# A first batch's token mix written straight to three rank groups, x added by TensorE, V as one piece, and a new order table

## The chip, the cores and the metric

The kernel runs on one core of one Trainium2 chip. The metric is the device time of one execution in microseconds (us). Engine names are those of the profile: PE is TensorE's matmul, PEld its weight load, DVE is VectorE, ACT ScalarE, POOL GpSimd, SP SyncE, which issues the DMAs.

## What is computed

The attention part is a recurrence over 768 positions for 4 batches and 8 heads of width 48; its result, with the heads side by side, is x with 384 channels. On x a mix over the positions of rank 32 and a feed-forward of width 1536 follow:

```python
for t in range(S):
    cur = np.einsum('bhd,bhe->bhde', u[None] * kt, vt)
    y[:, :, t] = np.einsum('bhd,bhde->bhe', rt, state + cur)
    state = wt[:, :, :, None] * state + np.einsum('bhd,bhe->bhde', kt, vt)
...
xt = x.transpose(0, 2, 1)
h = xt @ U @ V                      # U: 768 x 32, V: 32 x 768
u = x + h.transpose(0, 2, 1)
ch = np.maximum(u @ w_ch1, 0.0) @ w_ch2
return (u + ch)
```

## The kernel before

**Tiles and stages.** Each batch is cut into 6 chunks of 128 positions (chunks are numbered 0 to 23 through all batches) and into 2 blocks of 384 positions. All work is a list of named steps, and the string ORDER, which was written ahead of time, gives the order in which the steps are emitted. Every engine works through its own steps strictly in that order; a step that waits holds up all steps behind it on its engine. Three more digits of a step's entry choose between two engines where the step allows it, and how many dummy matmuls ("leads", in the function `warm`, L180) TensorE does ahead of it.

**A chunk** on its way: DVE scans the decays twice (F, L367, and Q, L380) with a reciprocal R between them; r and k are scaled (RP L387, KS L392, on DVE or POOL). For the first batch r times k is formed by PR (L448) and reduced by TensorE (MD); for later batches RK, RU and RED (L413, L416, L420) do this. TensorE makes the scores (AM, `aps`, L495), the diagonal comes from SEL and SEL2 (L430, L432), and DVE merges both with a predicated copy (CP, L498). KT, KN and DS (L482, L486, L505) make the chunk's contribution to the state, which ZA (L526) adds and ZM (L535, L537) decays. YA and YZ (L555 to L582) give the chunk's y in PSUM, XE (L598, ACT) copies it to `xT`, and XT and XN (L616, L620) turn it into `xn`, positions on partitions.

**The token mix of a batch** (`token_mix`). GA (L640) multiplies `xn` of the six chunks with U. The chunks c and c+4 go to the same 32 of 128 PSUM partitions, so that four partial sums of 32 ranks stand in `ga`. G4 (L646, ACT) copies them to SBUF, and SELM (L651, `gb`) adds the four with a matrix `sel` and puts the sum three times, on partitions 0, 32 and 64. GS (L655) rounds it to fp32r, and GSL (L660, DVE) puts the remainder in the third group.

**u of a block** (`make_u`). For each of 3 channel tiles HP (L690) multiplies `gs` with `Vst`, the three stacked groups of V (its second group holds V's remainder), UADD (L694, DVE) adds x in place in `xT`, UH (L699, ACT, or L701, DVE) rounds to fp32r in a tile `u`, and UL (L705, POOL or DVE) gives the remainder.

**The feed-forward of a block** (`ffn`). 12 tiles: UP (L738, 9 matmuls), HH (L745 or L747, relu and rounding), HL (L751, remainder). Then 3 output tiles of 36 matmuls each: DN (L774, in four parts of 9). O (L789, DVE) adds u, and OUT sends it. PSUM has three buffers `ffn` for `ga`, `gb`, `hp`, UP and DN.

**Weights** come as 64-bit words. For each piece LRAW loads it, AB and E (L261, L278, ACT) and C1, C2, C3 (L283, L290, L297, DVE) turn the bits, ADD (L304, POOL) joins them, and HI (L314, L316) and SUB (L321) split into fp32r and remainder. V is two pieces of 384 columns on 96 partitions, each loaded by three DMAs.

Of the kernel before, what the change touches and what calls it, by code (L numbers as in the profile page):

```python
# [37 lines left out]
def channel_order():  # L38
# [13 lines left out]
    "3n01g01F03p00004C01X03s03r04E03y03u03o03t03v01h01i04D01j01G04d01k00104e01I00201l01H05304F04L03q01Z01J04H01m0"  # L52
    "1K01n00z04G00301o10401Y01L03z11M00700503++3w01a04m04I01N15201b03-"
    "13x04014M042C4100+00604404304J00P00901000804K10-"
    "04605U01105B04R01c01204714g00R04n14S04h15504N04l15610A04i04V01d04504O04P14s01300G04W01e04j04X10h04804Q11f15T"
    "04k04T05700I05C14f04905804t00i04A00B01405u00k04B00C00j04o00l05c05W04w04p04q15D00m05X01515d16105Y05914U04r15b"
    "04u00Q05E05A00n05H04v00D00o00q04Y05I05Z00E01600S08O05i05a05400T00s05x04Z05j05e00U01805v05y14x05F04a05z08X00F"
    "05J05f14y10V04b05L00r05+00Y04z04c05G14+06218Y08o05V00p10W06304-08P05K06001705g18y01905k05-"
    "00a01A00t05O05h11B00u00X15P06405w08x00v05005l08p01C05Q05100w06511y05R05M05p05N02x05S08Z15m06618R06E08Q00H05q"
# [927 lines left out]
```

## Time and profile before

| what | value |
|---|---|
| median of 3 runs (lowest to highest) | 483.46 us (481.89 to 484.27) |
| the profiled execution's own time | 483.14 us |
| its span in the profile | 481.4 us |
| PE, PEld busy | 449.4 us (93%), 409.8 us (85%) |
| DVE, ACT, POOL busy | 314.6 us (65%), 171.2 us (36%), 119.9 us (25%) |
| first matmul of the feed-forward | 81.77 us after the span's start |
| DMA read | 41.94 MB |

The profile is of one execution. Busy shares are means over the whole span, and the stages differ: until the first feed-forward matmul the chunks of batch 0 and the first weights are prepared, and from then on feed-forward matmuls and the chunks of later batches share TensorE. A row of a timeline gives start, length, engine, line of code, operation and tiles; in square brackets stands the idle time before it and what ended it.

### The profile page before, as it was taken

The numbers are of one execution on the slowest core, as the hardware profiler recorded it, in microseconds if no ns is written. First come the engines' busy times: TensorE is split into PE (matmuls) and PEld (weight loads), VectorE is DVE, ScalarE is ACT, GpSimd is POOL, SyncE is SP. The second block draws the span as 40 slices with busy tenths as digits, with TensorE's granted clock in tenths as the row PEclk, the third lists the DMA queues.
The fourth block names the chain that finished last, engine by engine and source line by source line (L and its number), as shares of the span: only waits on it lengthen the run. The fifth ranks groups of instructions, "written<-read, shape, count | busy, mean of one in ns | idle before, by whom it ended". The sixth has DMA issues, their size and how long they took to land.

```text
span 481.4 us, 9783 instructions
## 1 busy us (share of the span) xinstructions
PE 449.4 (93%) x4041; PEld 409.8 (85%) x4041; DVE 314.6 (65%) x532; ACT 171.2 (36%) x446; POOL 119.9 (25%) x113
## 2 busy tenths in 40 slices
PE   7568797899999999999999999999999999999994
PEld 3357655799889889899999889799999899999994
DVE  8998999997999888967139558954134144422420
ACT  5485967874524532432044451320011121001000
POOL 3515422534643664402006050600000010000000
PEclk9786999999999999999999999999999999999999
DMA  8653867344105873214024360200000000000001
GB/s 301 226 193 93 298 212 252 116 146 157 38 23 154 251 216 90 75 43 130 18 83 149 100 218 34 84 20 1 33 18 0 19 17 18 0 34 16 1 17 39
DMA packets 20644, 47.38 MB, mean 98 GB/s; under 512 B 2480, under 2 KB 8880, under 8 KB 20592
## 3 DMA queue, kind: packets, MB, share of 16 engines
q1 hardware_dynamic: 20592, 46.67, 30.3%
q8 instruction: 34, 0.56, 0.5%
q14 instruction: 18, 0.15, 0.1%
HBM read 41.94 MB, written 4.72 MB: 97 GB/s over the span
## 4 chain that ended last, share of the span: by engine, by line
PE 70%; DVE 16%; DMA 5%; ACT 4%; issue 3%; POOL 1%; SPq 0%; ACTq 0%; DVEq 0%; POOLq 0%
PE f L774 29%; PE f L738 28%; PE aps L495 3%; DVE F L367 3%; DVE A L498 2%; DMA v<-in_vN 2%; PE y L555 2%; DVE cva_w L297 1%; DMA raw_w<-in_w 1%; PE trk L482 1%; DVE Q L380 1%; PE y L565 1%; PE trx L616 1%; DMA rk<-in_rkT 1%; DVE cva_w L283 1%
## 5 line engine op out<-in xcount | busy, mean ns | idle before, releaser
L738 PE MATMUL f<-u,w1h 128*128 128x384 f32 x576 | 157.0, 343 | 1.6 <-DVE u L705 0.8
L738 PEld LDWEIGHTS f<-u,w1h 128*128 128x128 f32 x576 | 105.3, 188 | 4.5 <-DVE u L705 1.5
L774 PE MATMUL f<-hh,w2h 128*128 128x384 f32 x288 | 99.4, 345 | 0.7 <-DVE hl L751 0.5
L774 PE MATMUL f<-hh,w2l 128*128 128x384 f32 x288 | 97.7, 339 | 0.7 <-POOL w2l L321 0.7
L738 PE MATMUL f<-u,w1l 128*128 128x384 f32 x288 | 97.5, 338 | 0.0
L751 DVE SCALAR_TENSOR_TENSOR hl<-f,hh 128x384 fp32r<-128x384 f32 x96 | 52.7, 552 | 34.9 <-ACT hh L745 33.7
L745 ACT ACTIVATE hh<-f 128x384 fp32r<-128x384 f32 x52 | 25.2, 486 | 137.6 <-PE f L738 137.5
L774 PE MATMUL f<-hl,w2h 128*128 128x384 f32 x288 | 66.7, 339 | 0.1
L774 PEld LDWEIGHTS f<-hh,w2h 128*128 128x128 f32 x288 | 54.1, 188 | 3.0 <-issue 1.0
L774 PEld LDWEIGHTS f<-hh,w2l 128*128 128x128 f32 x288 | 54.1, 188 | 1.2 <-POOL w2l L321 1.0
L738 PEld LDWEIGHTS f<-u,w1l 128*128 128x128 f32 x288 | 54.1, 188 | 0.0
L774 PEld LDWEIGHTS f<-hl,w2h 128*128 128x128 f32 x288 | 51.9, 188 | 0.5 <-DVE hl L751 0.4
L789 DVE TENSOR_TENSOR xT<-f,xT 128x384 f32<-128x384 f32 x24 | 13.3, 554 | 50.7 <-PE f L774 50.6
L747 DVE TENSOR_SCALAR hh<-f 128x384 fp32r<-128x384 f32 x44 | 24.2, 552 | 31.0 <-PE f L738 30.7
L430 ACT ACTIVATE A<-ident,dv 128x128 f32<-128x128 f32 x112 | 35.6, 392 | 24.8 <-PE y L565 16.1
L498 DVE COPY_PREDICATED A<-maskf,aps 128x1024 f32<-128x1024 uint32 x24 | 31.5, 1313 | 11.4 <-PE aps L495 5.7
L304 POOL TENSOR_TENSOR cva_w<-cva_w,raw_w 128x384 int32<-128x384 int32 x24 | 28.3, 1182 | 42.1 <-DVE cva_w L297 16.7
L432 POOL TENSOR_SCALAR_AFFINE_SELECT A<-dv 128x512 f32<-128x512 f32 x20 | 15.9, 804 | 75.5 <-PE y L565 58.9
L367 DVE TENSOR_TENSOR_SCAN F<-w,resets 128x517 f32<-128x517 f32 x24 | 33.4, 1399 | 1.8 <-POOL rk L392 1.3
L495 PE MATMUL aps<-rk 48*128 48x128 f32 x384 | 29.7, 297 | 3.8 <-DVE A L498 2.9
L380 DVE TENSOR_TENSOR_SCAN Q<-w,qd 128x516 f32<-128x516 f32 x24 | 32.5, 1354 | 0.1
L495 PEld LDWEIGHTS aps<-rk 48*128 48x128 f32 x384 | 25.0, 199 | 8.8 <-issue 3.7
(116 smaller groups left out, 575.7 us busy)
## 6 DMA issues: line engine op xcount, KB each, us to landing
rk<-in_rkT SPq DMA_DIRECT2D x24, 512.0 KB, 4.4
raw_w<-in_w SPq DMA_DIRECT2D x24, 384.0 KB, 4.2
kr<-in_rkN SPq DMA_DIRECT2D x18, 384.0 KB, 3.9
w<-in_wT SPq DMA_DIRECT2D x24, 258.5 KB, 2.8
v<-in_vN SPq DMA_DIRECT2D x24, 224.0 KB, 3.3
out_dram<-xT SPq DMA_DIRECT2D x24, 192.0 KB, 1.9
raw_V<-in_V SPq DMA_DIRECT2D x6, 96.0 KB, 4.2
raw_U<-in_U SPq DMA_DIRECT2D x1, 192.0 KB, 4.3
```

The costliest lines, as they stand in the source:

```text
L304: lambda: nc.gpsimd.tensor_tensor(out=d["to"].bitcast(I32), in0=d["a"].bitcast(I32), in1=d["e"], op=ALU.add),
L367: nc.vector.tensor_tensor_scan(out=F[:, ::-1], data0=st["w"][:, ::-1], data1=resets[:, ::-1], initial=1.0, op0=ALU.mult, op1=ALU.add)
L380: nc.vector.tensor_tensor_scan(out=st["Q"], data0=st["w"][:, 0:n], data1=qd, initial=0.0, op0=ALU.mult, op1=ALU.add)
L430: nc.scalar.activation(A[:, i, j], ident, AF.Copy, scale=dv[:, NP * i + j : NP * i + j + 1])
L432: nc.gpsimd.affine_select(out=A[:, i], in_=dv[:, NP * i : NP * i + NP].unsqueeze(2).broadcast_to([P, NP, P]), pattern=[[0, NP], [1, P]], c ...
L495: nc.tensor.matmul(aps[:, i, j, :], rk[r, 1, j, :], rk[r, 0, j, :], start=True, stop=True)
L498: nc.vector.copy_predicated(flat(st["A"]), mask8, flat(st["aps"]))
L738: nc.tensor.matmul(ps, wt[:, f, ct, :], u[ct][:, z], start=(n == 0), stop=(n == 8))
L745: nc.scalar.activation(hh, d["ps", f], AF.Relu)
L747: nc.vector.tensor_scalar(out=hh, in0=d["ps", f], scalar1=0.0, scalar2=None, op0=ALU.max)
L751: nc.vector.scalar_tensor_tensor(out=hl, in0=d["ps", f], scalar=0.0, in1=hh.bitcast(F32), op0=ALU.max, op1=ALU.subtract)
L774: nc.tensor.matmul(d["o", ct], wt[:, 4 * ct + part, f - 3 * part, :], hid[f][z], start=(part == 0 and n == 0), stop=(part == 3 and n == 8),)
```

## The change

**Token mix of batch 0.** GA, G4 and SELM of the first batch go. A step GW for each chunk multiplies `xn` with U three times, once for each of the three groups of `gb`, and adds up over the six chunks in PSUM. The other batches keep GA, G4 and SELM.

**u of block 0 of batch 0.** A step IX multiplies x with the identity into `hp`; HP then adds to it. UHP and ULP read `hp` in PSUM in place of `xT`, ULP is on DVE always, and XU copies `hp` to `xT` (ACT or DVE), which the output steps O wait for. The seven other blocks keep UADD, UH and UL.

**V** is one piece of 128 partitions and 192 columns, loaded by one DMA. VM copies it by identity matmuls into the three groups in PSUM (12 matmuls), HIV (ACT) rounds, SUBV (DVE) gives the remainder. HI and SUB of V go.

**`sel`** is made by three reductions instead of one and a copy.

**The order table** is new as a whole. Leads before: MD 0 31, KT 0 6, YA 5 22, XT 0.5 4, SELM 0 4, AM 6 2, YA 6 2, in all 71. Leads now: MD 0 31, YA 7 7, in all 38.

```diff
 ORDER = (
-    "3n01g01F03p00004C01X03s03r04E03y03u03o03t03v01h01i04D01j01G04d01k00104e01I00201l01H05304F04L03q01Z01J04H01m0"
...
+    "3i03k04700001S01J01b03n03j04803t04A04Z04+00200103m03p04G03o00303q04901U01T00403l04B04C01K00501V01L01M01W04Y0"
...
-    sel1 = const.tile([P, RANK], F32, name="sel1")
-    nc.vector.tensor_reduce(
-        out=sel1, in_=ident.rearrange("p (g r) -> p r g", r=RANK), op=ALU.add, axis=AX.X
-    )
-    nc.vector.tensor_copy(sel, sel1.unsqueeze(1).broadcast_to([P, 3, RANK]))
+    for i in range(3):
+        nc.vector.tensor_reduce(out=sel[:, i], in_=ident.rearrange("p (g r) -> p r g", r=RANK), op=ALU.add, axis=AX.X)
...
-            else:
-                for g in range(3):
-                    nc.sync.dma_start(flat[RANK * g : RANK * (g + 1), :], V[i].bitcast(U32))
+                nc.sync.dma_start(flat[:, 0 : 2 * NCH * RANK], (U if kind == "U" else V).bitcast(U32))
...
+                def spread(half=half):
+                    ps = d["ps", half] = psF.tile([P, TB], F32, tag="ffn", name=f"vm_{half}")
+                    lead(ps)
+                    for q in range(2):
+                        r = slice(RANK * (2 * half + q), RANK * (2 * half + q + 1))
+                        for g in range(3):
+                            nc.tensor.matmul(
+                                ps[RANK * g : RANK * (g + 1), cols * q : cols * (q + 1)], ident[:, r], d["a"],
+                                start=True, stop=True,
+                            )
+
+                def high_v(half=half, ts=ts):
+                    nc.scalar.activation(Vst[:, ts], d["ps", half][0 : 3 * RANK], AF.Copy)
+
+                def low_v(half=half, ts=ts):
+                    r = slice(RANK, 2 * RANK)
+                    nc.vector.tensor_tensor(
+                        out=Vst[r, ts], in0=d["ps", half][r], in1=Vst[r, ts].bitcast(F32), op=ALU.subtract
+                    )
...
+            def whole(c):
+                if c == 0:
+                    d["gb"] = psF.tile([P, DM], F32, tag="ffn", name=f"gb_{b}")
+                    lead(d["gb"])
+                for i in range(3):
+                    to = d["gb"][RANK * i : RANK * (i + 1), :]
+                    nc.tensor.matmul(to, U_sb[:, c, :], xns[b, c]["xn"], start=(c == 0), stop=(c == NCH - 1))
...
+            by_pe = (b, blk) == (0, 0)
+
+            def take_x(ct=ct):
+                hp = d["hp", ct] = psF.tile([P, TB], F32, tag="ffn", name=f"hp_{b}_{blk}_{ct}")
+                lead(hp)
+                nc.tensor.matmul(hp, ident, blocks[b, blk][:, ct, :], start=True, stop=False)
...
-                nc.tensor.matmul(hp, gs["gs"][:, cs], Vst[:, ts], start=True, stop=True)
+                nc.tensor.matmul(hp, gs["gs"][:, cs], Vst[:, ts], start=not by_pe, stop=True)
...
+            def keep(eng, ct=ct):
+                if eng == "ACT":
+                    nc.scalar.activation(blocks[b, blk][:, ct, :], d["hp", ct], AF.Copy)
+                else:
+                    nc.vector.tensor_copy(blocks[b, blk][:, ct, :], d["hp", ct])
...
-            o = step(f"O {b}.{blk}.{ct}", "DVE", total, [prev], use=[bps, bx])
+            o = step(f"O {b}.{blk}.{ct}", "DVE", total, [prev] + keeps, use=[bps, bx])
...
-    pieces = [("U", 0), ("V", 0)] + pieces[:8] + [("V", 1)] + pieces[8:]
+    pieces = [("U", 0), ("V", 0)] + pieces
```

What the new table does to the queues is seen at three places. The numbers in the names tell tiles apart: `hp_0_0_1` is batch 0, block 0, channel tile 1; `aps_7`, `y_7`, `Z_7` belong to chunk 7, the second of batch 1; `f1_0_0_0` is the first feed-forward tile.

On TensorE, right behind the token mix of batch 0, before (L495 is AM 6, L690 the three HP of block 0, L482 is KT 6):

```order
L495 MATMUL aps_6_961<-rk_6_660 128x128 x8
L690 MATMUL hp_0_0_0_976<-Vst_125,gs_0_958 128x384
L690 MATMUL hp_0_0_1_988<-Vst_125,gs_0_958 128x384
L690 MATMUL hp_0_0_2_990<-Vst_125,gs_0_958 128x384
L482 MATMUL trk_6_992<-ident_101,rk_6_660 128x128 x4
```

and now (L734 is IX, L743 HP, L507 KT, L520 AM, L530 DS, L641 XT):

```order
L743 MATMUL hp_0_0_0_864<-Vst_125,gs_0_1023 128x384
L743 MATMUL hp_0_1_0_1041<-Vst_125,gs_0_1023 128x384
L743 MATMUL hp_0_1_1_1045<-Vst_125,gs_0_1023 128x384
L743 MATMUL hp_0_1_2_1054<-Vst_125,gs_0_1023 128x384
L734 MATMUL hp_0_0_1_1064<-xT_0_0_395,ident_101 128x384
L743 MATMUL hp_0_0_1_1064<-Vst_125,gs_0_1023 128x384
L507 MATMUL trk_7_1068<-ident_101,rk_7_715 128x128 x4
L520 MATMUL aps_7_1081<-rk_7_715 128x128 x8
L530 MATMUL dS_120<-v_7_905,kn_7_1079 48x48 x8
L641 MATMUL trx_1_0_1106<-ident_101,xT_1_0_1091 128x128 x3
```

HP of block 1 now stands between the first and the second HP of block 0, and KT, AM and DS of chunk 7 behind them.

On TensorE, ahead of the first feed-forward matmul, before (y_6 and dS are of chunk 6):

```order
L555 MATMUL y_6_1002<-A_6_912,v_6_797 32x128 x8
L565 MATMUL y_6_1002<-A_6_912,v_6_797 32x128 x8
L616 MATMUL trx_1_0_1051<-ident_101,xT_1_0_1038 128x128 x3
L505 MATMUL dS_120<-v_6_797,kn_6_1044 48x48 x8
L738 MATMUL f1_0_0_0_1069<-u_0_0_0_1032,w1h_126 128x384
L738 MATMUL f1_0_0_0_1069<-u_0_0_0_1032,w1l_127 128x384
L738 MATMUL f1_0_0_0_1069<-u_0_0_1_1042,w1h_126 128x384
```

and now (the four rows of y_7 are YA 7 and YZ 7; L734 and L743 are IX and HP of the third channel tile; L507 is KT 8):

```order
L580 MATMUL y_7_1124<-A_7_989,v_7_905 32x128 x8
L590 MATMUL y_7_1124<-A_7_989,v_7_905 32x128 x8
L603 MATMUL y_7_1124<-rk_7_715,Z_6_1025 32x128 x8
L607 MATMUL y_7_1124<-rk_7_715,Z_6_1025 32x128 x4
L734 MATMUL hp_0_0_2_1172<-xT_0_0_395,ident_101 128x384
L743 MATMUL hp_0_0_2_1172<-Vst_125,gs_0_1023 128x384
L507 MATMUL trk_8_1185<-ident_101,rk_8_869 128x128 x4
L803 MATMUL f1_0_0_0_1196<-u_0_0_0_1119,w1h_126 128x384
L803 MATMUL f1_0_0_0_1196<-u_0_0_0_1119,w1l_127 128x384
L803 MATMUL f1_0_0_0_1196<-u_0_0_1_1149,w1h_126 128x384
```

Chunk 7, which came among the feed-forward matmuls before, now stands ahead of the first of them, and so does KT 8.

On DVE, before, from GSL of batch 0 (L660) to the second UL (L705); L694 is UADD:

```order
L660 TENSOR_TENSOR gs_0_958<-gb_0_949,gs_0_958 32x384
L420 TENSOR_REDUCE dv_7_974<-kr_7_671 128x8
L403 RECIPROCAL qd_109<-F_7_935 128x4
L498 COPY_PREDICATED A_6_912<-maskf_106,aps_6_961 128x1024
L694 TENSOR_TENSOR xT_0_0_415<-hp_0_0_2_990,xT_0_0_415 128x384
L694 TENSOR_TENSOR xT_0_0_415<-hp_0_0_1_988,xT_0_0_415 128x384
L694 TENSOR_TENSOR xT_0_0_415<-hp_0_0_0_976,xT_0_0_415 128x384
L420 TENSOR_REDUCE dv_8_1030<-kr_8_896 128x8
L380 SCALAR_TENSOR_TENSOR Q_7_1036<-w_7_648,qd_109 128x516
L705 TENSOR_TENSOR u_0_0_0_1032<-xT_0_0_415,u_0_0_0_1032 128x384
L705 TENSOR_TENSOR u_0_0_1_1042<-xT_0_0_415,u_0_0_1_1042 128x384
```

and now, the last twelve rows up to the third ULP (L761); ten rows stand between GSL and these, the first XU, two UADD of block 1, KS 7, RP 7 and weight work among them (L392 is F, L523 CP, L551 ZA, L747 UADD of block 1, L346 SUB):

```order
L392 SCALAR_TENSOR_TENSOR F_8_1093<-w_8_728,resets_87 128x517
L283 TENSOR_SCALAR cva_w2_2_1076<-cva_w2_2_1076 128x384
L428 RECIPROCAL qd_109<-F_8_1093 128x4
L523 COPY_PREDICATED A_7_989<-maskf_106,aps_7_1081 128x1024
L551 TENSOR_TENSOR Z_7_1121<-dS_120,Z_6_1025 128x384
L761 TENSOR_TENSOR u_0_0_0_1119<-hp_0_0_0_864,u_0_0_0_1119 128x384
L290 SCALAR_TENSOR_TENSOR cva_w2_2_1076<-raw_w2_2_1021,cva_w2_2_1076 128x384
L761 TENSOR_TENSOR u_0_0_1_1149<-hp_0_0_1_1064,u_0_0_1_1149 128x384
L747 TENSOR_TENSOR xT_0_1_717<-hp_0_1_2_1054,xT_0_1_717 128x384
L392 SCALAR_TENSOR_TENSOR F_9_1179<-w_9_953,resets_87 128x517
L346 TENSOR_TENSOR w1l_127<-cva_w1_4_872,w1h_126 128x384
L761 TENSOR_TENSOR u_0_0_2_1191<-hp_0_0_2_1172,u_0_0_2_1191 128x384
```

GSL and the last remainder of u were 13 rows apart on DVE with GSL counted, and are now 23, with the scans of chunks 8 and 9 and CP 7 between them.

More of the change, by code (lines that the diff above doesn't have):

```diff
@@ L310, in split_raw @@
             ready[key] = [add]
+            return
+        if kind == "V":
+            for half in range(2):
+                bps = Buf("ffn")
+                ts = slice(half * TB, (half + 1) * TB)
+                def spread(half=half):
[15 more added lines that the diff above has]
+                    )
+                vm = step(f"VM V{half}", "PE", spread, [add], take=[bps], use=[bcva])
+                hi = step(f"HIV V{half}", "ACT", high_v, [vm], use=[bps])
+                sub = step(f"SUBV V{half}", "DVE", low_v, [hi], use=[bps])
+                ready["V", half] = [hi, sub]
             return
@@ L660, in low @@
             nc.vector.tensor_tensor(out=gs[r], in0=d["gb"][r], in1=gs[r].bitcast(F32), op=ALU.subtract)
+        if b == 0:
+            sums, ga = [], None
+            def whole(c):
[5 more added lines that the diff above has]
+                    nc.tensor.matmul(to, U_sb[:, c, :], xns[b, c]["xn"], start=(c == 0), stop=(c == NCH - 1))
+            for c in range(NCH):
+                ga = step(
+                    f"GW {b}.{c}", "PE", lambda c=c: whole(c), xns[b, c]["steps"] + ready.get(("U", 0), []) + [ga],
+                    take=[bgb] if c == 0 else [], use=[bgb, xns[b, c]["buf"]],
+                )
+            hi = step(f"GS {b}", "ACT", high, [ga], take=[d["buf"]], use=[bgb])
+            d["step"] = step(f"GSL {b}", "DVE", low, [hi], use=[bgb, d["buf"]])
+            return
         ga = [
@@ L713, in make_u @@
-            xs = [s for c in range(3 * blk, 3 * blk + 3) for s in xns[b, c]["steps"] + xs_done.get((b, c), [])]
-            ad = step("UADD " + nm, "DVE", add, [hp] + xs, use=[bhp, bx])
-            uh = step(
-                "UH " + nm, "ACT", high, [ad] + ups[-1:], take=[bu], use=[bx], alt="DVE"
-            )
+                ENG[eng].tensor_tensor(out=u[:, 1], in0=summed(), in1=u[:, 0].bitcast(F32), op=ALU.subtract)
+            def keep(eng, ct=ct):
[3 more added lines that the diff above has]
+                    nc.vector.tensor_copy(blocks[b, blk][:, ct, :], d["hp", ct])
@@ new lines, in make_u @@
+            nm = f"{b}.{blk}.{ct}"
+            xs = [s for c in range(3 * blk, 3 * blk + 3) for s in xns[b, c]["steps"] + xs_done.get((b, c), [])]
+            if by_pe:
+                ix = step("IX " + nm, "PE", take_x, xs + [hp], take=[bhp], use=[bx])
+                hp = step("HP " + nm, "PE", mix, [gs["step"], ix] + ready.get(("V", blk), []), use=[bhp, gs["buf"]])
+                uh = step("UHP " + nm, "ACT", high, [hp] + ups[-1:], take=[bu], use=[bhp], alt="DVE")
+                ul = step("ULP " + nm, "DVE", lambda low=low: low("DVE"), [uh], use=[bhp, bu])
+                keeps.append(step("XU " + nm, "ACT", keep, [hp] + xs, use=[bhp, bx], alt="DVE"))
+            else:
+                hp = step(
+                    "HP " + nm, "PE", mix, [gs["step"], hp] + ready.get(("V", blk), []), take=[bhp], use=[gs["buf"]],
+                )
+                ad = step("UADD " + nm, "DVE", add, [hp] + xs, use=[bhp, bx])
+                uh = step("UH " + nm, "ACT", high, [ad] + ups[-1:], take=[bu], use=[bx], alt="DVE")
+                ul = step("UL " + nm, "Pool", low, [uh], use=[bx, bu], alt="DVE")
@@ L718, in make_u @@
             ups.append(uh)
-            ul = step("UL " + nm, "Pool", low, [uh], use=[bx, bu], alt="DVE")
             d["uhs"].append(uh)
@@ L860, in general @@
         recurrence(xs)
-        del steps[:], ups[:]
+        del steps[:], ups[:], keeps[:]
         with tc.For_i(0, B, 1) as b:
```

132 lines of the change are left out of this document (65 added, 67 removed).

## The prediction

> **What bounds the kernel now.** I read the busy slices of the page first (40 slices of 12 us, in tenths), then a table of windows, then the timeline where the feed-forward begins.
>
> ```profile
> PE   7568797899999999999999999999999999999994
> DVE  8998999997999888967139558954134144422420
> PEclk9786999999999999999999999999999999999999
> ```
>
> There are two regimes. Up to about 82 us DVE is full and PE has holes; from then on PE is full. PEclk is the granted clock of PE; it dips in the first 60 us only. The windows give the sizes (length, then the busy time of PE, PEld, DVE, ACT, POOL with counts, PE clock, DMA share, GB/s):
>
> ```profile
> 3.61:74.96 71.35, 56.31 (x671) 39.76 (x671) 66.28 (x105) 50.19 (x139) 26.91 (x24) 0.86 0.67 225
> 74.96:82.05 7.09, 4.54 (x76) 3.50 (x73) 7.02 (x13) 5.91 (x17) 2.96 (x3) 1.00 0.66 219
> 82.00:100.00 18.00, 15.93 (x144) 14.72 (x144) 17.36 (x39) 13.63 (x35) 7.13 (x6) 1.00 0.44 152
> 100.00:130.00 30.00, 29.00 (x190) 27.33 (x189) 26.92 (x53) 16.64 (x38) 14.66 (x13) 1.00 0.39 122
> 130.00:160.00 30.00, 29.54 (x283) 27.47 (x282) 28.30 (x42) 11.35 (x32) 14.92 (x14) 1.00 0.33 96
> 160.00:200.00 40.00, 39.14 (x457) 34.65 (x457) 35.50 (x57) 16.50 (x44) 21.18 (x19) 1.00 0.56 166
> 200.00:476.00 276.00, 274.23 (x2238) 262.12 (x2234) 131.34 (x223) 56.99 (x143) 31.11 (x29) 1.00 0.15 48
> ```
>
> From 3.61 to 74.96 DVE is busy for 66.28 of 71.35 us: DVE sets when GSL of batch 0 comes, not the length of the token-mix chain. From 82 to 200 us PE idles for 118 - 15.93 - 29.00 - 29.54 - 39.14 = 4.39 us, afterwards almost never (1.77 of 276). So the time is the start of the feed-forward, plus the PE work that is then left, plus a few us of PE idle, plus a fixed end. What the change is worth is the sum of the shifts of the first three. The timeline at the hand-over:
>
> ```profile
> 74.96 0.56 DVE L660 TENSOR_TENSOR gs<-gb,gs 32x384 fp32r<-32x384 f32 x1
> 75.55 0.55 DVE L420 TENSOR_REDUCE dv<-kr 128x8 f32<-128x384 f32 x1
> 75.61 0.79 PE L690 MATMUL hp<-Vst,gs 96*128 96x384 f32 x3
> 76.02 0.17 DVE L403 RECIPROCAL qd<-F 128x4 f32<-128x4 f32 x1
> 77.43 1.48 DVE L694 TENSOR_TENSOR xT<-hp,xT 128x384 f32<-128x384 f32 x3
> 78.82 0.55 DVE L420 TENSOR_REDUCE dv<-kr 128x8 f32<-128x384 f32 x1
> 79.27 1.23 DVE L380 TENSOR_TENSOR_SCAN Q<-w,qd 128x516 f32<-128x516 f32 x1
> 80.41 1.01 DVE L705 TENSOR_TENSOR u<-xT,u 128x384 fp32r<-128x384 f32 x2
> 81.77 0.44 PE L738 MATMUL f<-u,w1h 128*128 128x384 f32 x1
> ```
>
> GSL starts at 74.96, the first feed-forward matmul at 81.77, 6.81 us later. Rows overlap by some 0.09 us, so I cost a step by start to start.
>
> **What moves ahead of GSL, on DVE.** 105 steps stand ahead of it before, 114 now. Unit prices are from this piece of queue (RP 0.60, C2 0.27, CP 1.19, C3 0.46) and the scan above (79.27 to 80.41, 1.14):
>
> ```profile
> 64.89 0.68 DVE L387 TENSOR_TENSOR rk<-rk,Q 128x512 f32<-128x512 f32 x1
> 65.49 0.35 DVE L290 TENSOR_SCALAR cva_w<-cva_w 128x384 uint32<-128x384 uint32 x1
> 65.76 1.28 DVE L498 COPY_PREDICATED A<-maskf,aps 128x1024 f32<-128x1024 uint32 x1
> 66.95 0.54 DVE L297 SCALAR_TENSOR_TENSOR cva_w<-raw_w,cva_w 128x384 uint32<-128x384 uint32 x1
> 67.41 0.54 DVE L420 TENSOR_REDUCE dv<-kr 128x8 f32<-128x384 f32 x1
> ```
>
> Any other step 384 wide I take at 0.46, any 512 wide at 0.60. Counted from the orders: one more weight piece, C1, C2, C3, +1.00; V at half the width, about -0.3; one CP more (that of chunk 6) +1.19; one Q +1.14; one HI +0.46; two SUBV +0.92; four KS more +2.40; one PR and two RP fewer -1.80; RU and ZM one fewer, RED one more, -0.46. Sum +4.55. POOL has 25 steps ahead instead of 23, and POOL costs DVE time:
>
> ```profile
> 13.12 1.23 POOL L392 TENSOR_TENSOR rk<-rk,F 128x512 f32<-128x512 f32 x1 [0.80 <-DVE kr L448]
> 13.23 1.67 DVE L387 TENSOR_TENSOR rk<-rk,Q 128x512 f32<-128x512 f32 x1
> ```
>
> The same RP that took 0.68 above takes 1.67 beside a POOL step. Two more such steps cost between 0 and 2.0; I take 0.45, since the POOL step must fall on a step that it blocks. [...] GSL thus starts at 74.96 + 4.55 + 0.45 = 80.0.
>
> What shortens the mix does not help there: G4 and SELM leave the chain, but GSL waits for its place in DVE's queue.
>
> ```profile
> 71.85 0.49 ACT L646 ACTIVATE g<-ga 128x384 f32<-128x384 f32 x1 [0.48 <-PE ga L640]
> 72.41 0.87 PE L651 MATMUL gb<-g,sel 128*96 128x384 f32 x2
> 73.12 0.49 PE L180 MATMUL aps<-resets 128*128 128x384 bf16 x2
> 73.86 0.46 ACT L655 ACTIVATE gs<-gb 96x384 fp32r<-96x384 f32 x1
> ```
>
> GS was done at 74.32 and GSL started 0.64 later. PE's own additions (18 GW, 12 VM, one IX ahead) are at most one `gb` (0.71, 72.41 to 73.12) for each group of three, and at least an `hp` (0.26); 6 GW, 4 VM groups and 3 IX make 3.4 to 9.2 us. They are hidden as long as PE has room in this stage: it is busy for 56.31 of 71.35, and among that are 36 leads (KT 0, YA 5, XT 0.5, SELM) that the change takes out. If that cover were gone, the first y of each chunk would come later, and CP, which waits for AM on PE, is what DVE would then wait for.
>
> **From GSL to the first feed-forward matmul.** Now DVE does GSL 0.59, RED 0.47, XU 0.46, two UADD 0.93, KS 0.60, SUB 0.46, HI 0.46, RP 0.60, SUB 0.46, C1 0.27, F 1.14, C2 0.27, R 0.09, CP 7 1.19, in all 7.99, before PE may do YA 7, YZ 7, IX, HP and KT 8. XU has no row; it copies 384 from PSUM, between 0.38 (ACT's like copy less overlap) and UADD's 0.46, and I take the latter. IX lies between 0.26 and 0.71, taken at 0.65, nearest the other fp32 matmul. PE's rows, and what is moved:
>
> ```profile
> 92.54 1.16 PE L495 MATMUL aps<-rk 48*128 48x128 f32 x16
> 93.63 0.45 PE L738 MATMUL f<-u,w1h 128*128 128x384 f32 x1
> 96.77 0.64 PE L555 MATMUL y<-A,v 128*32 128x128 f32 x16 [1.28 <-DVE A L498]
> 98.44 0.44 PE L738 MATMUL f<-u,w1h 128*128 128x384 f32 x1
> 106.81 0.60 PE L482 MATMUL trk<-ident,rk 128*128 128x128 f32 x4
> 107.17 0.42 PE L774 MATMUL f<-hh,w2h 128*128 128x384 f32 x1
> 109.00 0.56 PE L505 MATMUL dS<-v,kn 128*48 128x48 f32 x16
> 109.50 0.44 PE L774 MATMUL f<-hh,w2h 128*128 128x384 f32 x1
> ```
>
> YA and YZ 1.67, IX 0.65, HP 0.26, KT 0.36: 2.94. With 0.1 for each of two hand-offs and 0.4 for a POOL step that blocks, 11.5. The feed-forward starts at 91.5 instead of 81.77, **+9.7**. The 7 leads of YA 7 run while CP 7 is awaited.
>
> **What is then no longer to do.** AM 7 1.09, YA and YZ 7 1.67, two KT 0.72, DS 7 0.50, three HP of block 1 0.79: **-4.8**.
>
> **PE idle behind it.** Before, PE stood for 1.28 at the y of chunk 7, and for hl:
>
> ```profile
> 87.58 0.44 PE L738 MATMUL f<-u,w1h 128*128 128x384 f32 x1 [0.79 <-DVE hl L751]
> ```
>
> Chunk 7 is now done, more weight pieces too, and the remaining PE work is the same, so DVE has about 8 us more of lead. Between 0 and all 4.39 I take **-3.0**, the two waits and the smaller ones up to 130.
>
> Small things: V's DMA shrinks from 6 of 96 KB to one of 192 KB, and no DVE wait above hangs on it; the other two XU are on ACT (50.19 of 71.35 busy), and O, which waits for them, comes 30 us later; `sel` takes one reduction more ahead of the first scan, at a place where DVE waits for a DMA.
>
> **Sum**, on the profiled execution's 483.14 (0.32 below the median of 483.46): 483.14 + 9.7 - 4.8 - 3.0 = **485.0**. Within 0.5% of the median, 481.0 to 485.9, is what a measurement can hardly tell from no change.
>
> **Rivals.**
> (a) DVE's stalls and blockings grow with the longer queue. They were 5.07 idle and the blocked steps; if GSL shifts by a further 2.5 and half as much idle is saved (1.5), 489.0. For it: nine more steps, and the first SUB now stands close behind its ADD on POOL. Against: the ZA steps stand, by my count along the queues, 1 us or more behind what they need.
> (b) The clock. Rows of a window where PE had little work:
>
> ```profile
> 36.00:38.00 2.00, 1.59 (x8) 1.50 (x8) 2.00 (x5) 2.00 (x8) 0.00 (x0) 0.50 0.72 272
> ```
>
> The clock fell to 0.50, and 33 leads are taken out. At half clock YA 7 to KT 8 cost 2.9 more, and the first 2 us of feed-forward, one such window, 1.0: 488.9. [...] Against: GW, VM and IX are real work in the leads' place, and 7 leads stand right ahead.
> (c) Faster: DVE's stalls in the first stage go. If 4.0 of the 5.07 idle us vanish, GSL comes at 76.0 and the feed-forward at 87.5; with all 4.39 of PE's idle saved the time is 483.14 + 5.7 - 4.8 - 4.4 = 479.6. It decides from a GSL at about 78. For it: by the orders, AM of the early chunks now stands ahead of KT and DS, so that CP would wait less for fresh scores. Against: nothing removes the blockings by POOL.
> (d) The shortened mix sets the start after all (no DVE bound): then G4 and SELM, 0.49 + 0.71, come off the path and nothing is lost: about 482, inside the band.
>
> **Chances.** Forecast 0.45 (two thirds within the band, one third above), (a) 0.15, (b) 0.08, (c) 0.22, (d) 0.10. Faster 0.22; same 0.30 + 0.10 = 0.40; slower 0.15 + 0.15 + 0.08 = 0.38. The likeliest case alone spans 483 to 487.5. For 8 in 10 the range reaches to (c) and (a): 479.5 to 489.2.
>
> **What would show it.** GSL (then L685) starting near 80 and the first feed-forward matmul (L803) near 91.5 with chunk 7's y just ahead; under 2 us of PE idle from there to 200 us; PEclk at 9 from 60 us on. It is wrong if GSL comes before 78 (DVE did not bound as I say), or if PE idles after the start as before.

## The result, and the profile after

The changed kernel takes 481.09 us (median of 16 runs, 478.29 to 483.01) against 483.42 for the kernel before (16 runs, 481.45 to 488.17) on the same chip: a ratio of 0.9944, 95% interval 0.9921 to 0.9967. Timed twice more beside the experiments it came out at 0.9921 (0.9888 to 0.9954) and 0.9932 (0.9908 to 0.9956). It is faster by 0.6 to 0.8%; the forecast was 485.0. The profiled execution took 481.94, with a span of 480.2. The slices of its page:

```profile
PE   7497988999999999999999999999999999999994
DVE  7898789999989999854996496433333255403410
PEclk9757879999999999999999999999999999999998
```

The windows, from DVE's first scan to GSL, to the first feed-forward matmul, and on (columns as in the prediction's table):

```profile
3.61:79.21 75.60, 62.88 (x743) 44.66 (x741) 65.57 (x114) 53.38 (x154) 29.27 (x25) 0.77 0.66 219
79.21:90.26 11.05, 9.11 (x124) 6.47 (x117) 10.96 (x21) 10.47 (x32) 4.82 (x6) 1.00 0.65 243
90.26:100.00 9.74, 9.27 (x67) 8.68 (x66) 9.74 (x23) 6.37 (x14) 3.01 (x3) 1.00 0.47 141
100.00:130.00 30.00, 29.27 (x242) 27.37 (x241) 27.68 (x54) 14.05 (x30) 13.84 (x14) 1.00 0.41 129
130.00:160.00 30.00, 30.00 (x270) 28.14 (x269) 27.80 (x44) 14.29 (x42) 14.08 (x11) 1.00 0.35 112
160.00:200.00 40.00, 40.00 (x406) 36.64 (x405) 38.63 (x60) 15.62 (x42) 12.85 (x12) 1.00 0.46 139
```

DVE is busy for 65.57 of 75.60 us ahead of GSL: the nine more steps cost no busy time at all, but its idle time has doubled, from 5.07 to 10.03. Behind the start PE idles for 0.47 + 0.73 us up to 200 us, where it had idled for 4.39. The hand-over, from the timeline:

```profile
76.83 1.38 DVE L523 COPY_PREDICATED A<-maskf,aps 128x1024 f32<-128x1024 uint32 x1
76.94 0.85 PE L696 MATMUL gb<-xn,U_sb 128*32 128x384 f32 x6
77.54 1.27 ACT L455 ACTIVATE A<-ident,dv 128x128 f32<-128x128 f32 x4
78.71 0.47 ACT L680 ACTIVATE gs<-gb 96x384 fp32r<-96x384 f32 x1
79.21 0.56 DVE L685 TENSOR_TENSOR gs<-gb,gs 32x384 fp32r<-32x384 f32 x1 [1.00 <-ACT gs L680]
79.83 0.79 PE L743 MATMUL hp<-Vst,gs 96*128 96x384 f32 x3 [0.48 <-DVE gs L685]
90.26 0.42 PE L803 MATMUL f<-u,w1h 128*128 128x384 f32 x1
91.67 0.44 PE L803 MATMUL f<-u,w1h 128*128 128x384 f32 x1 [0.47 <-ACT u L755]
```

GSL does not wait for its place in the queue: DVE stands idle for 1.00 us ahead of it, for the `gs` that ACT writes. That `gs` comes late is not the doing of the mix's matmuls alone: the last GW ends at 77.79, but ACT works without a gap on KN 6 and on SEL 7 (the row L455), which stand ahead of GS in its order, and GS starts at 78.71, 0.9 later. So ACT's queue is the last to hold GSL up. The first run with added leads, below, shows the same 0.9 (75.76 to 76.68), and the other two profiles of the changed kernel show DVE idle for 1.04 and 1.07 ahead of GSL, for the same `gs`; no run moved GS ahead of SEL 7. For the whole stretch behind the start, one window each of before and after (up to 474):

```profile
81.77:474.00 392.23, 386.76 (x3298) 365.53 (x3295) 239.10 (x407) 115.33 (x292) 89.00 (x79) 1.00 0.24 74
```
```profile
90.26:474.00 383.74, 381.70 (x3204) 362.65 (x3202) 235.24 (x406) 106.60 (x273) 66.58 (x60) 1.00 0.23 71
```

and PE's last feed-forward rows, of before and of after:

```profile
474.61 0.69 PE L774 MATMUL f<-hl,w2h 128*128 128x384 f32 x3
```
```profile
473.20 0.69 PE L839 MATMUL f<-hl,w2h 128*128 128x384 f32 x3
```

The last matmul thus ends at 475.30 before and at 473.89 now. From the start to there it was 393.53 us and is 383.63, of which PE's idle fell from 5.47 to 1.93 (-3.5) and its work from 388.06 to 381.70 (-6.4). With the start +8.5 later that makes -1.4; the profiled times differ by -1.2.

### The profile page after: what moved, and what is told of

Same layout as the page of the kernel before. It is cut to its first block, busy times and chain, and to the rows that moved or that the text cites. A ratio compares the mean times of both kernels' runs of the same rounds, so it can differ in the third digit from the quotient of the medians.

```text
span 480.2 us, 9825 instructions
## 1 busy us (share of the span) xinstructions
PE 454.2 (95%) x4060; PEld 414.0 (86%) x4060; DVE 314.5 (65%) x549; ACT 170.4 (35%) x457; POOL 101.7 (21%) x97
## 4 chain that ended last, share of the span: by engine, by line
PE 81%; DVE 7%; ACT 4%; DMA 4%; issue 2%; SPq 1%; POOL 0%; DVEq 0%; ACTq 0%
PE f L839 32%; PE f L803 31%; PE aps L520 4%; DMA raw_w<-in_w 2%; PE y L580 2%; PE trx L641 2%; PE trk L507 2%; PE dS L530 2%; PE y L590 1%; PE y L603 1%; DMA w<-in_wT 1%; ACT A L455 1%; DVE F L392 1%; DVE A L523 1%; PE ga L665 1%
## 5 line engine op out<-in xcount | busy, mean ns | idle before, releaser
L803 PE MATMUL f<-u,w1h 128*128 128x384 f32 x576 | 155.4, 341 | 0.8 <-ACT u L755 0.5
L810 ACT ACTIVATE hh<-f 128x384 fp32r<-128x384 f32 x42 | 20.6, 490 | 117.3 <-PE f L803 117.2
L812 DVE TENSOR_SCALAR hh<-f 128x384 fp32r<-128x384 f32 x54 | 29.8, 553 | 31.3 <-PE f L803 31.1
L455 ACT ACTIVATE A<-ident,dv 128x128 f32<-128x128 f32 x132 | 41.8, 394 | 22.8 <-PE y L590 10.1
L523 DVE COPY_PREDICATED A<-maskf,aps 128x1024 f32<-128x1024 uint32 x24 | 32.3, 1347 | 6.5 <-PE aps L520 3.3
L520 PE MATMUL aps<-rk 48*128 48x128 f32 x384 | 32.5, 316 | 4.4 <-POOL cva_w L297 2.3
L520 PEld LDWEIGHTS aps<-rk 48*128 48x128 f32 x384 | 27.5, 216 | 10.4 <-issue 3.1
L457 POOL TENSOR_SCALAR_AFFINE_SELECT A<-dv 128x512 f32<-128x512 f32 x15 | 12.9, 862 | 107.3 <-PE y L590 96.5
L297 POOL TENSOR_TENSOR cva_w<-cva_w,raw_w 128x384 int32<-128x384 int32 x24 | 29.6, 1244 | 26.2 <-DVE cva_w L290 16.7
L392 DVE TENSOR_TENSOR_SCAN F<-w,resets 128x517 f32<-128x517 f32 x24 | 32.4, 1358 | 0.3 <-DMA w<-in_wT 0.3
L405 DVE TENSOR_TENSOR_SCAN Q<-w,qd 128x516 f32<-128x516 f32 x24 | 30.4, 1268 | 0.0
```

The lines of the kernel that those rows point to most:

```text
L297: lambda: nc.gpsimd.tensor_tensor(out=d["to"].bitcast(I32), in0=d["a"].bitcast(I32), in1=d["e"], op=ALU.add),
L392: nc.vector.tensor_tensor_scan(out=F[:, ::-1], data0=st["w"][:, ::-1], data1=resets[:, ::-1], initial=1.0, op0=ALU.mult, op1=ALU.add)
L405: nc.vector.tensor_tensor_scan(out=st["Q"], data0=st["w"][:, 0:n], data1=qd, initial=0.0, op0=ALU.mult, op1=ALU.add)
L455: nc.scalar.activation(A[:, i, j], ident, AF.Copy, scale=dv[:, NP * i + j : NP * i + j + 1])
L520: nc.tensor.matmul(aps[:, i, j, :], rk[r, 1, j, :], rk[r, 0, j, :], start=True, stop=True)
L523: nc.vector.copy_predicated(flat(st["A"]), mask8, flat(st["aps"]))
```

## The experiments

Twelve runs on three occasions, on three chips, each beside the kernel before; medians of different occasions stand on different chips, so the ratios are the safer measure between them. "Start" is the first feed-forward matmul of the profiled execution, "behind" the time from it to the end of the last matmul there.

| kernel | median, us (runs) | ratio to before (95%) | GSL | start | behind |
|---|---|---|---|---|---|
| before | 483.42 (16) | 1 | 74.96 | 81.77 | 393.53 |
| changed, first | 481.09 (16) | 0.9944 (0.9921-0.9967) | 79.21 | 90.26 | 383.63 |
| changed, second | 480.28 (8) | 0.9921 (0.9888-0.9954) | 77.02 | 88.69 | 383.52 |
| changed, third | 481.71 (6) | 0.9932 (0.9908-0.9956) | 78.28 | 90.09 | 383.55 |
| old mix | 479.98 (6) | 0.9905 (0.9880-0.9931) | 77.85 | 88.90 | 383.22 |
| old u | 482.57 (12) | 0.9967 (0.9946-0.9988) | 78.67 | 90.83 | 384.27 |
| both old | 482.54 (12) | 0.9984 (0.9958-1.0010) | 77.08 | 89.94 | 383.83 |
| chunk 7 late | 485.69 (12) | 1.0020 (0.9993-1.0047) | 78.26 | 81.03 | 396.45 |
| 42 leads added | 480.28 (6) | 0.9913 (0.9884-0.9941) | 77.18 | 89.10 | 382.10 |
| the same again | 479.19 (6) | 0.9893 (0.9868-0.9919) | 76.65 | 88.57 | 382.90 |
| old mix, 42 leads | 482.86 (12) | 0.9966 (0.9940-0.9992) | 79.55 | 90.96 | 383.49 |
| 40 old leads back | 485.69 (12) | 1.0032 (1.0004-1.0061) | 81.82 | 92.88 | 383.70 |
| 22 of them | 484.62 (12) | 1.0000 (0.9976-1.0023) | 81.02 | 92.31 | 383.82 |
| before, 40 leads out | 486.52 (12) | 1.0034 (1.0006-1.0062) | 76.79 | 85.37 | 393.92 |

The three rows of the changed kernel are the first reading: what lies behind the start is the same within 0.1 us; the start itself wanders by 1.6 us between executions of one program. In the edited versions of the changed kernel the line numbers are smaller by ten (L675 is its L685). No run took back V as one piece or `sel` alone, so what these two are worth is not shown.

**The old mix.** GA in two pieces, G4 and SELM in place of the six GW. (Two expectations below say that the old mix goes over DRAM. It does not: G4 copies the four partial sums from PSUM to SBUF.)

```diff
-        if b == 0:
+        if b == -1:
             sums, ga = [], None
 order:
-GW 0.0 to GW 0.5
+GA 0.0 at GW 0.3's place, GA 0.1 and G4 0 at GW 0.5's, SELM 0 ahead of YA 6
```

> The changed kernel with the first batch's token mix as before (GA at the places of the fourth and sixth GW, then G4 and SELM), all else and its order kept. In the changed kernel DVE stood idle for 1.00 us at GSL, released by GS. If the short mix is part of the gain (theory A), G4 and SELM put back come at the end of that path: GSL 1.2 us later, near 80.4, first feed-forward matmul near 91.4, time 482.3. If the new places of the steps make the gain alone (theory B), the six GW are 3 us of PE work less, GSL stays within 0.4 of 79.2, and the time within 0.5 of 481.1.

Neither forecast came: GSL stands at 77.85 and the time is 479.98. The run did not get slower; 0.9905 is at the fast edge of the changed kernel's intervals. But its mix chain is the longer one, as theory A has it:

```profile
74.00 0.84 PE L655 MATMUL ga<-xn,U_sb 128*32 128x384 f32 x4
77.85 0.56 DVE L675 TENSOR_TENSOR gs<-gb,gs 32x384 fp32r<-32x384 f32 x1 [2.82 <-ACT gs L670]
```

From the end of the last GA (74.84) to GSL it is 3.01 us here; from the end of the last GW to GSL it is 1.42 in the first profile of the changed kernel, and 1.42 again in the first run with 42 leads. At the full clock (1.00 in the windows of all three stretches) the old chain is thus 1.6 us longer. DVE waits 2.82 us at GSL here, 1.00 in the changed kernel's first profile, and still comes 1.36 earlier than there (0.83 later than in the second). Windows of the first and the second profile of the changed kernel and of this one show where that is from:

```profile
46.00:50.00 4.00, 4.00 (x48) 2.51 (x46) 2.58 (x5) 1.82 (x6) 2.06 (x3) 0.50 0.46 128
50.00:54.00 4.00, 4.00 (x79) 3.11 (x79) 1.87 (x4) 2.98 (x10) 0.78 (x1) 0.87 0.47 90
```
```profile
46.00:50.00 4.00, 4.00 (x72) 2.96 (x71) 3.28 (x6) 2.46 (x8) 2.06 (x3) 0.81 0.45 129
50.00:54.00 4.00, 4.00 (x99) 2.97 (x95) 3.17 (x6) 4.00 (x13) 0.41 (x1) 1.00 0.72 224
```
```profile
46.00:50.00 4.00, 3.92 (x74) 2.70 (x73) 3.97 (x6) 3.09 (x10) 2.32 (x3) 1.00 0.64 184
50.00:54.00 4.00, 3.76 (x95) 2.78 (x93) 3.69 (x6) 4.00 (x14) 0.59 (x1) 1.00 0.87 269
```

At a granted clock of 0.50 (0.87 in the second window) PE does 48 and 79 matmuls in 4 us instead of 74 and 95, and DVE, which waits there for dS (1.41 and 0.78) and for ACT's rounding of V (1.34), is busy for 2.58 and 1.87 us instead of 3.97 and 3.69. So by the time alone the clock hides what the chain costs. It must be held still before the times of the two mixes can be compared; the runs with leads below do that for the most part.

**The old u.** x of the first block added by DVE (UADD, UH, UL).

```diff
-            by_pe = (b, blk) == (0, 0)
+            by_pe = (b, blk) == (-1, 0)
 order:
-IX 0.0.0 to 0.0.2; UHP, ULP, XU of the three channel tiles
+UADD, UH, UL in their places
```

> The changed kernel with block 0 of batch 0 by UADD, UH and UL as before (no IX, no XU), order kept, UADD at the places of XU. A: three UADD on DVE instead of one XU there, 0.9 us more on DVE ahead of the first feed-forward matmul, and UH waits for UADD: start near 91.3, time 482.2. B: DVE's order there is set by CP 7 and not by u, so that the start stays at 90.3 +- 0.4 and the time at 481.1 +- 0.5.

482.57: slower than the changed kernel by 0.9 to 2.3 us, whichever of its three medians is taken, though its interval (0.9946 to 0.9988) overlaps theirs. From GSL to the start it is 12.16 us (11.05, 11.67 and 11.81 in the changed kernel), behind the start 0.7 more. The clock may have part in it, at 0.86 where the changed kernel has 1.00 in all three profiles:

```profile
78.67:90.83 12.16, 9.47 (x116) 6.66 (x113) 11.87 (x22) 10.47 (x32) 4.79 (x6) 0.86 0.57 215
```

The medians are on the side of theory A (482.2); the start, 90.83, lies between the two forecasts. How much of it DVE's extra steps cost, and how much PE's lower clock beside them, this run doesn't part.

**Chunk 7 late.** The u of block 0 and four UP are pulled ahead of the work of chunk 7 and of block 1, so that the feed-forward starts early, as it did before.

```diff
 GSL 0
+the u of block 0; then UP 0, 1, 3, 5 with their HH, HL, between the steps below
 HP of block 1, KT 7, AM 7, YA 7, YZ 7
-YA 7 with 7 leads
+YA 7 with none
```

> The changed kernel with u of block 0 and the first four feed-forward tiles pulled ahead of chunk 7 and of block 1's HP, right behind GSL; the 7 leads of YA 7 taken out. B: the feed-forward starts 3 to 4 us earlier, near 86.5, but 4.8 us of PE work stand behind it and PE idles 2 to 3 us more up to 200 us, as in the kernel before: 482.5 to 484. A: where chunk 7 stands is worth nothing, the start and the work cancel: 481.1 +- 0.6, with under 1.5 us of PE idle behind the start.

485.69, 4.0 to 5.4 above the changed kernel. The start came at 81.03, 7.7 to 9.2 earlier, and what lies behind it grew by 12.9. Its window (up to 474) against that of the changed kernel shows PE's idle at 8.54 instead of 2.04, and more work:

```profile
81.03:474.00 392.97, 384.43 (x3285) 363.65 (x3286) 247.09 (x422) 115.73 (x298) 74.25 (x63) 1.00 0.23 73
```
```profile
103.17 0.66 PE L497 MATMUL trk<-ident,rk 128*128 128x128 f32 x4 [1.55 <-ACT xn L635]
111.29 0.44 PE L793 MATMUL f<-u,w1h 128*128 128x384 f32 x1 [2.70 <-DVE hl L806]
```

So in this order the early start bought nothing: the work returned behind it (387.9 us of PE's 396.45, against 381.7), and with it came the waits for hl and for the chunks' steps. Theory B has the direction but not the sizes: it gave a start near 86.5, 2 to 3 us more idle, where it is 6.5, and 482.5 to 484. Part of the loss belongs to the places that were picked for the pulled-up steps, since the kernel before idles by only 5.47 behind its start.

**42 leads added.** Matmuls whose result nobody reads, 16 ahead of MD 0, 13 ahead of AM 4, 4 ahead of XT 0.1, 9 ahead of XT 0.2.

```diff
+    for i in range(4):
+        step(f"WARM {i}", "PE", lambda i=i: lead(psF.tile([P, TB], F32, tag="ffn", name=f"warm_{i}")), take=[Buf("ffn")])
 order:
+WARM 0 (16) ahead of MD 0; WARM 1 (13) of AM 4; WARM 2 (4) of XT 0.1; WARM 3 (9) of XT 0.2
```

> The changed kernel with 42 leads more, in a spare PSUM buffer, where PE stood idle and the clock then fell to half: 16 ahead of MD 0, 13 ahead of AM 4, 4 ahead of XT 0.1, 9 ahead of XT 0.2. Theory C, the half clock in the first stage (mean 0.78 up to GSL) delays DS and AM, for which DVE then waits (1.41, 0.78, 1.34, 0.98 us): clock above 0.9 there, GSL near 76.5, first feed-forward matmul near 87.5, time 478.5. Against it (DVE's own queue sets GSL): GSL within 0.7 of 79.2 and 481.1 +- 0.6, or later, where the leads delay real work.

> The kernel with 42 added leads of the first set once more, beside the changed kernel on one chip: its 0.9913 stood against 0.9944 and 0.9921 of the changed kernel. If keeping TensorE at full clock from 43 us on is worth what the first profile says, 1 us faster than the changed kernel; if the runs spread by the clock's chance only, within 0.5 us of it. GSL 77.2 within 0.3 in its profile if the leads hold the clock.

Both profiles show a granted clock of 1.00 from 46 to 77 us, GSL stands at 77.18 and 76.65, and DVE waits at it for `gs` by 1.03 and 1.04. The time is 0.9913 and 0.9893 of before; in the second, beside the changed kernel's third run, 479.19 against 481.71. The first forecast of GSL at 76.5 and 478.5 was too bold by 0.7 and 1.8. The second forecast had 1 us faster than the changed kernel and GSL at 77.2; it came 2.5 faster, with GSL at 76.65. By the ratios the leads are worth 0.1 to 0.5% over the three runs of the changed kernel, and the intervals still touch (0.9868 to 0.9919 and 0.9908 to 0.9956), so the gain in time is likely but not shown beyond doubt.

**Old mix with the 42 leads.** The diffs of the two runs together.

> The changed kernel with the old mix of batch 0 (six partial sums gathered over DRAM in two pieces, one matmul) and with the 42 added leads of the run before this one, both at once. Each alone beat the changed kernel: 0.9905 and 0.9913 of the kernel before, against 0.9944. Theory M, the old mix is cheaper in itself (18 matmuls fewer on TensorE while its clock is half): the two gains add, GSL about 76, the first feed-forward matmul about 88, time 479. Theory C, the old mix only happened to keep TensorE at full clock between 44.6 and 51.5 us (0.52 us of DVE idle there against 3.80), and its longer chain costs 1.8 us at the gate (an idle of 2.82 ahead of it against 1.00): with the leads the clock is full there anyway, so only the cost of the chain is left: GSL about 78.5, start 90.3, time 481.3.

482.86, and by the medians 2.6 to 3.7 us slower than the same leads with the new mix (by the ratios 2.6 to 3.5). Both stand at full clock (1.00) from 46 to 76 us; the row at the gate, of this run and of the 42 leads alone:

```profile
79.55 0.56 DVE L675 TENSOR_TENSOR gs<-gb,gs 32x384 fp32r<-32x384 f32 x1 [2.65 <-ACT gs L670]
```
```profile
77.18 0.56 DVE L675 TENSOR_TENSOR gs<-gb,gs 32x384 fp32r<-32x384 f32 x1 [1.03 <-ACT gs L670]
```

This is theory C in kind, and more than its 78.5 and 481.3: GSL is 2.4 later, 1.6 of it in the wait for `gs`. The two gains do not add; the old mix was not cheaper in itself, it had met a better clock. Not all of the 2.4 is the chain's length: behind PE's holes ahead of `gb` (0.58 and 1.08) the clock fell once more at 77 us, to 0.50 up to 80, and `gb` took 1.59 there where it takes 0.89 at 1.00 in the run of the old mix alone. That leaves some 1.7 for the chain, near the 1.6 from the rows above. Without leads its worth can't be told from the clock's by the time alone.

**The old order's 40 leads back, then 22 of them.**

```diff
 order (leads):
-KT 0: 0, YA 5: 0, XT 0.5: 0, KT 6: 0, AM 6: 0, YA 6: 0
+KT 0: 6, YA 5: 22, XT 0.5: 4, KT 6: 4, AM 6: 2, YA 6: 2   (second run: YA 5: 22 alone)
```

> The changed kernel with the leads (matmuls whose result nobody reads, in front of a step that waits) that the old order had and the new one dropped: 6 before KT 0, 22 before YA 5, 4 before XT 0.5, 4 before KT 6, 2 before AM 6, 2 before YA 6, 40 more in all. Theory C (half clock in the first stage costs DVE's waits for TensorE): the stage at half clock between 62 and 68 us goes, GSL 0.7 earlier, time 480.3. Rival, TensorE's clock there is off the path: 481.1, or slower by the leads' own 2 to 4 us where they stand in front of work that is ready.

> The changed kernel with only the 22 leads in front of YA 5 that the old order had there; the other 18 of the run with 40 leads stay out. Theory L, in the new order these stand in front of work that is ready, and the gate's chain waits behind them: they took 3.74 us of TensorE from 67.88 in that run, GSL stood at 81.82 against 77.0 and 79.2; so GSL about 80.5, 484. Rival, all 40 leads share the loss by their number: 22 of 40 of 4.6, 2.5 us, 483.2.

The first expectation of theory C (480.3) failed: 485.69, slower by 5.4 than the changed kernel on the same occasion. These leads stand where the old order had them, those of SELM 0 ahead of KT 6. The timeline of that run:

```profile
67.13 0.91 PE L724 MATMUL hp<-xT,ident 128*128 128x384 f32 x2
67.88 3.74 PE L173 MATMUL y<-resets 128*128 128x384 bf16 x22
71.54 0.65 PE L570 MATMUL y<-A,v 128*32 128x128 f32 x16
```

The 22 leads hold PE for 3.66 us with no idle on either side, and GW of the last chunks queues behind them. Alone they bring GSL to 81.02 and the time to 484.62, 2.9 more than the changed kernel beside it. The time does not part theory L from its rival (a share by number, 2.5); that GSL comes within 0.8 of that with all 40 speaks for L. The whole gain of the change would be gone if the new order had kept these leads.

**The kernel before without its 40 leads** (all but the 31 ahead of MD 0).

```diff
 order (leads):
-KT 0: 6, YA 5: 22, XT 0.5: 4, SELM 0: 4, AM 6: 2, YA 6: 2
+0 at each
```

> The kernel before, its order untouched, with 40 of its 71 leads left out (all but the 31 ahead of MD 0). Theory C: the stage up to the gate loses time to half clock, 485 to 486 against 484. Rival, the leads are worth nothing there: within 0.5 of the kernel before.

486.52, slower by 0.06 to 0.62%. Its window and that of the kernel before at the same place:

```profile
70.00:74.00 4.00, 3.39 (x15) 0.87 (x7) 3.99 (x8) 2.47 (x7) 1.41 (x1) 0.50 0.86 262
74.00:78.00 4.00, 3.42 (x19) 2.18 (x18) 2.34 (x6) 1.47 (x4) 2.61 (x3) 0.50 0.17 69
```
```profile
70.00:74.00 4.00, 3.38 (x12) 0.95 (x12) 4.00 (x9) 2.46 (x7) 1.04 (x1) 1.00 0.87 312
74.00:78.00 4.00, 3.04 (x41) 2.49 (x45) 3.91 (x8) 2.18 (x7) 2.84 (x3) 1.00 0.18 40
```

The clock is at half (0.50 where it was 1.00), the start 3.6 later (8.58 after GSL instead of 6.81). Theory C, a little beyond its 485 to 486: here the leads did pay. In the new order the same 22 stand between rows without idle and cost 3.66 us; here, ahead of YA 5, they end before the row they stand in front of can start:

```profile
62.97 3.74 PE L180 MATMUL y<-resets 128*128 128x384 bf16 x22
67.10 0.65 PE L555 MATMUL y<-A,v 128*32 128x128 f32 x16 [0.39 <-DVE A L498]
```

**The changed kernel again, twice.**

> The changed kernel unaltered, profiled once more and timed beside the other three. If the half clock falls by the program (theory C), TensorE stands at half clock again near 45 to 51 and 62 to 68 us, and DVE waits there about 3.8 us between 38 and 54; GSL 79.2 within 0.4. If it falls by chance, the stretches differ from the first profile's, and GSL with them by a us or more. Ratio to the kernel before 0.994.

> The changed kernel unaltered, third profile. Its GSL was at 79.21 and 77.02 in two executions, with half clock from 44.6 to 51.5 in the first and to about 47 in the second. If the time goes with that, span 478.0 to 480.5 and GSL between 76.5 and 79.5, again the later the longer the half clock lasts between 38 and 54 us. Ratio 0.992 to 0.995.

Neither program nor chance alone: by windows of 1 and 2 us, one stretch of half clock (0.50) ends near 51, 47.5 and 45 us in the three profiles, and a second lies near 61 to 68, 58 to 65 and 59 to 69. GSL moves between 77.02 and 79.21. That it comes the later the longer the half clock lasts up to 54 us does not hold: the third was at full clock from 46 us, and lost its time afterwards:

```profile
66.00:70.00 4.00, 4.00 (x69) 2.88 (x65) 1.94 (x6) 1.60 (x5) 0.23 (x1) 0.65 0.24 62
```

Here DVE is busy for 1.94 of 4 us, where the second profile has 3.82 at a clock of 1.00.

**Both old pieces.** The diffs of the old mix and of the old u together, in the new order.

> The changed kernel with both of its new pieces of arithmetic taken back, the mix of batch 0 over DRAM (as in old_mix) and x of the first block added by DVE (as in old_u); V as one piece and the new order stay. Theory O, the order of the table is what gains: 0.990 to 0.996 of the kernel before, 480 to 482, with the first feed-forward matmul near 90. Rival, the new pieces carry the gain: no faster than the kernel before, 484. By the two runs with one piece back each (0.9905 and 0.9967 against 0.9944 and 0.9921 of the changed kernel) 0.993 to 0.996.

0.9984, its interval holding 1: the new order without the new arithmetic can't be told from the kernel before. Theory O is too simple, and the sum of the two single runs (0.993 to 0.996) was too low; that the new pieces carry the gain is not excluded. Behind the start it has all of the gain (383.83), but the start comes 12.86 after GSL, 1.81 more than in the old-mix run and at a clock of 0.73 instead of 1.00; between the two medians lie 2.6 us. That is again the old u, or the clock beside it.

## Why the prediction was wrong

The frame held: start of the feed-forward, work left, idle, fixed end. Its sum missed the profiled 481.94 by 3.1: 1.2 at the start, 1.6 in the work, 0.5 in the idle, less 0.2 at the end. That turned the sign: the sum set +9.7 at the start against -7.8 behind it, the profiles have +8.5 against -9.9.

What of the change makes the gain is known in part. Behind the start, every version with the new order has 382.1 to 384.3 us, and those with chunk 7 among the feed-forward matmuls have 393.5 to 396.5: that part is the place of the work. The start takes 7 to 9 us of it back. There the new mix is worth 1.6 us of chain; the new u some 2.6 us by the medians, of which the clock may have a share.

**GSL at 80.0, the step that failed in its reason.** It came at 79.2, and at 77.0 and 78.3 in the other executions. "GSL waits for its place in DVE's queue" is wrong for the changed kernel: its three profiles show DVE idle for 1.00, 1.04 and 1.07 us ahead of GSL, waiting for `gs`, which itself stood 0.9 us in ACT's queue in the first. The +4.55 for more steps and +0.45 for POOL assumed the old prices; in fact busy time fell by 0.71 with nine more steps. The same two weight steps, C1 and C2, from the groups of before and of after:

```profile
L283 DVE TENSOR_SCALAR cva_w<-cva_w 128x384 f32<-128x384 f32 x11 | 6.6, 602 | 1.3 <-ACT cva_w L261 1.2
L290 DVE TENSOR_SCALAR cva_w<-cva_w 128x384 uint32<-128x384 uint32 x11 | 5.1, 461 | 0.0
```
```profile
L276 DVE TENSOR_SCALAR cva_w<-cva_w 128x384 f32<-128x384 f32 x12 | 4.6, 388 | 1.7 <-ACT cva_w L258 1.7
L283 DVE TENSOR_SCALAR cva_w<-cva_w 128x384 uint32<-128x384 uint32 x12 | 4.1, 355 | 0.0
```

At 388 and 355 ns instead of 602 and 461, eleven pairs give back 3.5 us. POOL was not less busy (29.27 against 26.91), so what changed is where its steps fall. Before, five of the 22 C1 and C2 took 0.79 to 1.41 us in place of 0.35, and each of them began while a POOL step ran; now only one of the 24 is as long (0.81 at 39.03, also beside POOL; a step at 60.35 beside a POOL select kept its 0.35). One of the five:

```profile
33.24 1.22 POOL L387 TENSOR_TENSOR rk<-rk,Q 128x512 f32<-128x512 f32 x1 [8.34 <-DVE Q L380]
33.34 1.33 DVE L283 TENSOR_SCALAR cva_w<-cva_w 128x384 f32<-128x384 f32 x1
```

That the new table spares them is read from these two traces; no run moved a POOL step. The idle that I held fixed at 5.07 grew to 10.03. By the profile's releasers 3.2 of it ended with PE and 6.7 with ACT, and the ZA steps, which by my count stood 1 us or more behind what they need, waited 2.2 for dS. Part of the growth may go with the clock, 0.77 on the mean up to GSL: in the first run with the 42 leads the idle there is 6.7, at 0.84. Two errors of 5 us cancelled; that GSL was 0.8 off is luck and says little for the step.

**"What shortens the mix does not help"**: refuted by the rows (3.01 against 1.42 us from the last matmul with U to GSL) and by the runs with 42 leads, 2.6 to 3.7 us apart. **The stretch of 11.5** from GSL to the start: 11.05, 11.67, 11.81, right. **The start, +9.7**: +8.5, +6.9, +8.3.

**No longer to do, -4.8: the mis-sized term.** It measured -6.4. By groups AM gave 1.2, the y 2.1, KT 0.7, dS 0.9 and HP 0.7, in all 5.6; I had priced the y by starts (1.67) and one dS group (0.50, for 16 matmuls; the window has 20 fewer, as it also cut the end of chunk 6's). The other 0.8 is spread over what is left, the feed-forward matmuls above all.

**PE's idle, -3.0**: -3.5, right in kind and near in size. With the work it makes -9.9 behind the start where I had -7.8, the same within 0.1 in all three executions. (The bound on PE's additions, which is in no sum, speaks of one IX ahead and prices three.)

**The rivals.** (a) had the stalls right, but the blockings (DVE steps that take longer beside a POOL step) fell, and 489.0 did not come. (b) had the right agent in the wrong place: from GSL to the start the first profile shows 1.00; half clock struck earlier, among others at 44 to 51 and 60 to 68 us, where the page's slices show 7, 8 and 7, and "9 from 60 us on" was wrong. (Its row at 36 to 38 us is no case of little work: PE is busy there for 1.59 of 2.00 us.) (c) had the direction, by a mechanism that did not happen (DVE's idle grew); its fork at 78 lies in the middle of the executions. (d) was nearest in its number, about 482, and had 0.10; that is luck too, since it had nothing lost and GSL 1.2 earlier, where GSL came 4.3 later and the gain lies behind the start. Given the 0.40 for no change and 0.38 for slower, the direction was missed; the time lay in the range.

## What to carry to other kernels

An engine that is 93% busy ahead of a step need not be what the step waits for: look at the row of that step itself, and at the row of the step it waits for (here GS, which stood in ACT's queue), and ask again for the changed order, because blocking, stalls and the bound all move with it. Compare two variants of a stage with the granted clock at hand; here the old mix read as no slower without leads and as some 3 us slower with them. Put a filler matmul where TensorE would stand anyway (here 22 of them cost 3 us in front of ready work), and price a move by what lies behind the moved start (here steady to 0.1 us) apart from the start (which wanders by 1.6).

## What was unexpected of the hardware

In these traces the granted clock does not follow from how busy PE looks. In the first profile of the changed kernel:

```profile
26.00:30.00 4.00, 4.00 (x32) 3.74 (x36) 4.00 (x6) 4.00 (x15) 0.97 (x1) 0.50 0.28 72
30.00:34.00 4.00, 4.00 (x56) 3.46 (x49) 4.00 (x7) 3.23 (x11) 1.18 (x1) 0.50 0.43 125
```

PE is busy for all of 8 us and stays at 0.50. Nor is it the same from one execution to the next: one stretch at half clock (0.50) ends near 51, 47.5 and 45 us in the three profiles of one program, whose GSL stands at 79.21, 77.02 and 78.28. What sets these stretches, and which instructions the granted clock goes by, no run here told apart.
